# Transposed x by crossbar from HBM, weights on a second queue, z on VectorE, query normalization moved forward, LN2 sums from accumulators

## The chip, the cores and the metric

The kernel runs on one core of one Trainium2 chip. The metric is the device time of one execution in microseconds (us), as the median of several runs. The span of a profile, from the first to the last instruction, is 1.7 us shorter than the time of the same run. Engine names: PE (TensorE matmul), PEld (its weight load), DVE (VectorE), ACT (ScalarE), POOL (GpSimd), SP (the sync engine, here a DMA queue). SBUF is the on-chip memory that tiles lie in, PSUM the one that matmuls write to. A "crossbar" load or transpose is a DMA that transposes a tile on its way (DMA_TRANSPOSE in the profile). In a profile line, L608 is line 608 of the kernel, and `a<-b` says that tile a is made from b; "landing" is the moment when a DMA is complete.

## The reference, cut to what matters

```python
x = A_x                                            # [1, 2048, 640] bf16
g = sigmoid((x * gate_w).sum(-1, keepdims=True))
qkv = x @ wqkv                                     # 32 heads of 20
pq, pk = phi(q), phi(k)
kv  = einsum("bhsd,bhse->bhde", pk, v)
z   = einsum("bhsd->bhd", pk)                      # sum of pk over all 2048 tokens
o   = (pq @ kv) / ((pq * z).sum(-1) + 1e-6)
a   = o @ wo
h   = gelu(layernorm(x) @ w1)                      # LN1, W1
x1  = x + shifted(h) @ w2                          # W2
b   = x1 + gelu(layernorm(x1) @ w3) @ w4           # LN2, W3, W4
out = g * a + (1 - g) * b
```

## The kernel before

Tokens are worked on in 16 tiles of 128. The stages on PE are: Q and K (x^T times wq and wk), G (x^T pk, from which kv is made), W1, W2, W3, then per tile "A" (normalized queries times M) and W4. Each engine gets its own instruction list. The lists are made before the run by a list scheduler in the kernel's Python: it assigns a cost in ns to each instruction, simulates, and places the next item where it thinks that it can start. PE then executes that order whatever really happens (the wait of 6.39 us below shows it). The parts that matter here:

```python
def t_x(t):                     # transpose one tile of x on PE, copy PSUM -> SBUF on DVE
    b = bank()
    tr_group(b, [x_tok[:, t, 128 * k:128 * (k + 1)] for k in range(KD)])
    copy(dve, xT[:, :, 128 * t:128 * (t + 1)], psb(b, 0, D).rearrange(...))

# head loads, all on SP: rows of x, wq, rows of x, wq, wk, gate vector ...
dma_in(x_tok[:, 0:2, :], ...); load_wq(0); load_wq(1); dma_in(x_tok[:, 2:4, :], ...)
...                             # q_two: tiles 0 and 1 together, one k-slice of wq at a time
for c in range(1, NCH):         # tiles 4..15: load rows, then crossbar SBUF -> SBUF
    dma_in(x_tok[:, 4 * c:4 * c + 4, :], ...)
    for t in range(4 * c, 4 * c + 4):
        sch.dma("sp", xT[:, :, 128 * t:128 * (t + 1)], x_tok[:, t, :], ..., transpose=True)

def z_add(t):                   # 16 adds on POOL, after LN1
    tt(pool, zacc[:, :] if t < NT - 1 else zsum[:, :], zacc[:, :], pk_tok[:, t, :], ALU.add)

def zb_group():                 # PE: broadcast the sum to all partitions with a matmul of ones
    b = pair()
    mm_group(ps[:, b, 0:512], [(ones_c[:, 0:128], zsum[:, 0:512])])
    mm_group(ps[:, b + 1, 0:128], [(ones_c[:, 0:128], zsum[:, 512:D])])
    copy(dve, zb[:, :], psf[:, 512 * b:512 * b + D])
# qn_tile: five DVE instructions normalize one tile of queries with zb, then a crossbar transpose
IT.add("MISC", ("w4load",), 0.0, w4_load, deps=[(("kvt", 1), 0.0), (("t1", NT - 1), 0.0), (("z", NT - 1), 1.5)])
```

The buffer of w4 shares memory with pk_tok, so w4 can be loaded only after z is done.

## Time and profile before

| | before |
|---|---|
| time, median | 268.6 us |
| span | 267.0 us |
| PE busy | 259.9 us |
| first K tile starts | 12.56 us |
| last matmul ends | 264.19 us |

The busy table of the page:

```profile
PE 259.9 (97%) x1727; PEld 136.4 (51%) x1727; DVE 154.2 (58%) x308; ACT 95.1 (36%) x184; POOL 101.2 (38%) x153
```

PE has little idle time to give, and the other engines are far from full. The waits of PE (engine, line, what it waited for, us in total, times, longest):

```profile
PE ps L608 <- DMA pqnT<-pq_tok: 1.6, 1, 1.6
PE ps L827 <- POOL ones_c L662: 1.6, 1, 1.6
PE ps L850 <- DMA wq<-in_A_wqkv_dram: 0.7, 1, 0.7
PE ps L850 <- DVE xT L668: 0.4, 1, 0.4
```

Only the first, third and fourth could go with this change. The timeline of PE shows where the K stage starts, and the later G and W1 groups (start us, us, instructions merged):

```profile
12.56 1.75 PE L608 MATMUL ps<-wkg,xT 128*128 128x512 bf16 x11
...
70.00 1.52 PE L778 MATMUL ps<-pk_tok,x_tok 128*128 128x512 bf16 x10
71.35 1.24 PE L608 MATMUL ps<-xnT,w_61 128*128 128x512 bf16 x5
```

The z sum before (groups of instructions: busy us, mean ns of one, idle before), and the one kind of DVE reduction that this trace contains:

```profile
L636 POOL TENSOR_TENSOR zacc<-zacc,pk_tok 128x640 f32<-128x640 f32 x15 | 21.0, 1400 | 0.4
L1035 DVE TENSOR_REDUCE dnr<-qprod 128x32 f32<-128x640 f32 x16 | 13.1, 820 | 0.5
```

The second line reads 640 numbers in 820 ns.

### The profile page before, as it was taken

The numbers are of one execution on the slowest core, as the hardware profiler recorded it, in microseconds if no ns is written. First come the engines' busy times: TensorE is split into PE (matmuls) and PEld (weight loads), VectorE is DVE, ScalarE is ACT, GpSimd is POOL, SyncE is SP. The second block draws the span as 40 slices with busy tenths as digits, with TensorE's granted clock in tenths as the row PEclk, the third lists the DMA queues.
The fourth block names the chain that finished last, engine by engine and source line by source line (L and its number), as shares of the span: only waits on it lengthen the run. The fifth ranks groups of instructions, "written<-read, shape, count | busy, mean of one in ns | idle before, by whom it ended". The sixth has DMA issues, their size and how long they took to land.

```text
span 267.0 us, 4369 instructions
## 1 busy us (share of the span) xinstructions
PE 259.9 (97%) x1727; PEld 136.4 (51%) x1727; DVE 154.2 (58%) x308; ACT 95.1 (36%) x184; POOL 101.2 (38%) x153
## 2 busy tenths in 40 slices
PE   7899999999999999999999999799999999999995
PEld 3555555555454546554444555354544555545553
DVE  1597877830005667995009957879733753766533
ACT  1396677743443552614555300003322302130000
POOL 5003995756579294965950020210103010030200
PEclk9999999999999999999999999999999999999999
DMA  6755997647768211415369510411701121110411
GB/s 180 262 90 138 185 196 135 189 84 116 101 125 267 96 39 35 87 27 64 76 128 311 52 25 3 49 25 25 150 0 27 30 97 27 20 29 0 125 49 49
DMA packets 50292, 24.78 MB, mean 93 GB/s; under 512 B 41692, under 2 KB 48861, under 8 KB 50272
## 3 DMA queue, kind: packets, MB, share of 16 engines
q1 hardware_dynamic: 49120, 21.23, 36.1%
q0 software_dynamic: 1152, 3.28, 5.3%
q8 instruction: 13, 0.21, 0.4%
q14 instruction: 7, 0.06, 0.1%
HBM read 12.04 MB, written 2.62 MB: 55 GB/s over the span
## 4 chain that ended last, share of the span: by engine, by line
PE 93%; DMA 3%; DVE 2%; SPq 1%; issue 0%
PE ps L608 62%; PE ps L1096 20%; PE ps L778 8%; DMA wq<-in_A_wqkv_dram 2%; DMA pqnT<-pq_tok 1%; PE ps L1078 1%; PE ps L1026 1%; PE ps L850 1%; SPq L283 1%; PE ps L929 1%; DVE x_tok L642 1%; DVE dnr L1035 0%; DVE pq_tok L1040 0%; DVE qprod L636 0%; PE ps L619 0%
## 5 line engine op out<-in xcount | busy, mean ns | idle before, releaser
L659 ACT ACTIVATE h2T<-ps 128x512 bf16<-128x512 f32 x52 | 31.1, 597 | 84.4 <-PE ps L608 84.4
L1096 PE MATMUL ps<-w_86,h2T 128*128 128x512 bf16 (+1 forms) x416 | 58.9, 299 | 0.0
L608 PE MATMUL ps<-xnT,w_60 128*128 128x512 bf16 x260 | 58.7, 379 | 0.0
L630 POOL TENSOR_SCALAR abx<-x_tok,stg 128x640 f32<-128x640 bf16 x16 | 14.9, 935 | 109.1 <-DVE x_tok L642 60.0
L1096 PEld LDWEIGHTS ps<-w_86,h2T 128*128 128x128 bf16 x416 | 32.5, 98 | 27.6 <-issue 1.8
L608 PEld LDWEIGHTS ps<-xnT,w_60 128*128 128x128 bf16 x260 | 24.7, 98 | 27.5 <-DVE abx L642 0.3
L636 DVE TENSOR_TENSOR x_tok<-ps,x_tok 128x512 bf16<-128x512 f32 (+1 forms) x32 | 15.6, 486 | 33.7 <-PE ps L608 32.0
L642 DVE SCALAR_TENSOR_TENSOR x_tok<-ps,stg,abx 128x512 bf16<-128x512 f32 (+1 forms) x32 | 16.9, 548 | 31.2 <-PE ps L1096 31.2
L659 ACT ACTIVATE Er<-ps 128x640 bf16<-128x640 f32 x32 | 22.5, 705 | 19.2 <-PE ps L608 9.8
L659 ACT ACTIVATE hsT<-ps 128x512 bf16<-128x512 f32 (+1 forms) x32 | 18.9, 594 | 24.9 <-PE ps L608 24.5
L608 PE MATMUL ps<-M_sb,pqnT 128*128 128x512 bf16 (+1 forms) x160 | 23.9, 299 | 1.6 <-DMA pqnT<-pq_tok 1.6
L778 PE MATMUL ps<-pk_tok,x_tok 128*128 128x512 bf16 (+1 forms) x160 | 24.2, 299 | 0.0
L608 PE MATMUL ps<-wkg,xT 128*128 128x512 bf16 (+1 forms) x160 | 24.0, 299 | 0.0
L608 PE MATMUL ps<-w_62,hsT 128*128 128x512 bf16 (+1 forms) x160 | 23.9, 299 | 0.0
L608 PE MATMUL ps<-xnT,w_61 128*128 128x512 bf16 x100 | 23.9, 379 | 0.0
L642 DVE SCALAR_TENSOR_TENSOR abx<-ps,stg,abx 128x512 f32<-128x512 f32 (+1 forms) x32 | 17.5, 549 | 9.7 <-POOL abx L630 5.0
L636 POOL TENSOR_TENSOR zacc<-zacc,pk_tok 128x640 f32<-128x640 f32 x15 | 21.0, 1400 | 0.4
L608 PE MATMUL ps<-wq,xT 128*128 128x128 bf16 (+1 forms) x140 | 21.1, 299 | 0.0
L608 PEld LDWEIGHTS ps<-M_sb,pqnT 128*128 128x128 bf16 x160 | 12.9, 98 | 13.0 <-DMA pqnT<-pq_tok 1.8
L608 PEld LDWEIGHTS ps<-w_62,hsT 128*128 128x128 bf16 x160 | 13.1, 98 | 11.7
L608 PEld LDWEIGHTS ps<-wkg,xT 128*128 128x128 bf16 x160 | 12.9, 97 | 9.4
L778 PEld LDWEIGHTS ps<-pk_tok,x_tok 128*128 128x128 bf16 x160 | 12.6, 98 | 8.8
(70 smaller groups left out, 256.5 us busy)
## 6 DMA issues: line engine op xcount, KB each, us to landing
w_60<-in_B_w_dram SPq DMA_DIRECT2D x1, 2160.0 KB, 9.8
w_86<-in_B_w_dram SPq DMA_DIRECT2D x1, 2080.0 KB, 8.8
x_tok<-in_A_x_dram SPq DMA_DIRECT2D x3, 640.0 KB, 6.1
out_dram<-x_tok SPq DMA_DIRECT2D x3, 640.0 KB, 4.5
wq<-in_A_wqkv_dram SPq DMA_DIRECT2D x5, 160.0 KB, 4.7
wkg<-in_A_wqkv_dram SPq DMA_DIRECT2D x1, 800.0 KB, 7.5
wv<-in_A_wqkv_dram POOLq DMA_DIRECT2D x1, 800.0 KB, 5.4
wo_aug<-in_A_wo_dram POOLq DMA_DIRECT2D x5, 150.0 KB, 5.0
```

The lines of the kernel that those rows point to most:

```text
L283: return e.dma_start(out_ap, in_ap)
L608: ins = e.matmul(out_ap, l, r, start=(i == 0), stop=(i == n - 1))
L630: return engf(lambda e: e.tensor_scalar(out_ap, in_ap, s1, s2, op0, op1), rd, [out_ap], cost=cost)
L636: return engf(lambda e: e.tensor_tensor(out_ap, a, b_, op), [a, b_], [out_ap], cost=cost)
L642: return dve(lambda e: e.scalar_tensor_tensor(out_ap, in0, scalar, in1, op0, op1), rd, [out_ap], cost=cost)
L659: return act(lambda e: e.activation(out_ap, in_ap, func, bias=bias, scale=scale), rd, wr, cost=cost)
L778: ins = e.matmul(o, l, r, start=(t0 + q_ == 0), stop=(t0 + q_ == NT - 1))
L850: ins = e.matmul(o, l, r, start=(k == 0), stop=(k == KD - 1))
L929: ins = e.matmul(o, l, r_, start=st_, stop=sp_, skip_group_check=True)
L1026: ins = e.matmul(o, l, r, start=st, stop=sp)
L1078: ins = e.matmul(o, l, r, start=True, stop=False)
L1096: ins = e.matmul(o, l, r, start=False, stop=(i == KFF - 1))
```

## The change

Its intent: free PE from transposes in the head, take z off the POOL engine (1.40 us an add, z done at 136.6 us) so that queries can be normalized long before W4 needs them, and shorten the LN2 statistics on DVE. The diff, cut to its core (evictions in pairs of PSUM banks, the tail and bookkeeping are left out):

```diff
-    dma_in(x_tok[:, 0:2, :], x2[0:256, :]..., "x01")
-    ...  # x rows and wq, wk, gate vector, all on SP
+    def load_xT(t):
+        sch.dma("sp", xT[:, :, 128 * t:128 * (t + 1)], x2[128 * t:128 * (t + 1), :], "trx%d" % (t % 4), transpose=True)
+    for k in range(KD):
+        sch.dma("act", wq[:, k, :], A_wqkv[128 * k:128 * (k + 1), 0:D], "wq%d" % k)
+    sch.dma("act", wkg[:, :, 0:D], ...)
+    sch.dma("act", wkg[:, :, D + 2:D + 3], gate_w...)
+    for c in range(NCH):
+        for t in range(4 * c, 4 * c + 4):
+            load_xT(t)
+        dma_in(x_tok[:, 4 * c:4 * c + 4, :], ...)
-    NWARM = 5
-    NWARM2 = 2
+    NWARM = 8
-    def q_two(t0):    # tiles 0 and 1 in steps of wq
+    def q_first():    # tile 0 alone in steps of wq
@@
-    def z_add(t):
-        tt(pool, zacc[:, :] if t < NT - 1 else zsum[:, :], zacc[:, :], pk_tok[:, t, :], ALU.add)
+    def z_sum(g):
+        cs = slice(160 * g, 160 * (g + 1))
+        dve(lambda e: e.tensor_reduce(qprod[:, cs], pk_tok[:, :, cs].rearrange("p n d -> p d n"), AX.X, ALU.add),
+            ..., cost=2740.0)
+        if g == 3:
+            copy(dve, zsum[:, :], qprod[:, :])
@@ LN2
-        tt(dve, x_tok[:, t, 0:512], ...); tt(dve, x_tok[:, t, 512:D], ...); bn_stats; bn_stats; bn_aggr
+        stt(x_tok[:, t, :], psf[...], 1.0, x_tok[:, t, :], ALU.mult, ALU.add, accum=st2[:, 0, t:t + 1])
+    def w2_sq(t):
+        activation(junk[:, 0, :], x_tok[:, t, :], ACTF.Square, accum=st2[:, 1, t:t + 1])
@@ normalization of queries: now paced by W1 and W3 groups instead of W4 tiles; transposes after W2 and LN2
-        deps = [(("zb",), 1.0), (("q", max(t, 2)), 2.0), (("w2", NT - 1), 0.5)]
+        deps = [(("zb",), 1.0), (("q", t), 2.0)]
+        IT.add("QT", ("qt", t), ..., deps=[(("qn", t), 3.2), (("w2", NT - 1), 0.5), (("t2", NT - 1), 0.0)])
@@
-    w4load deps ... (("z", NT - 1), 1.5)
+    w4load deps ... (("z", 3), 1.5)
```

More of the change, by code (lines that the diff above doesn't have):

```diff
@@ L246, in simulate @@
             elif sem is not None and sem.startswith("d:"):
-                self.eng_free[eng] = t + (500.0 if eng == "sp" else 1000.0)
+                self.eng_free[eng] = t + (1000.0 if eng == "pool" else 500.0)
                 self.dma_free = max(self.dma_free, t) + nbytes / 330.0
@@ L480, in _build @@
     st2 = pa.alloc("st2", [128, 8, NT], F32)
-    bn2 = pa.alloc("bn2", [128, NT, 2], F32)
-    bns = pa.alloc("bns", [128, 4, 12], F32)
     stg = pa.alloc("stg", [128, 4, NT], F32)
@@ L499, in _build @@
     junk = pa.alloc("junk", [128, 1, D], BF16)
-    zacc = pa.alloc("zacc", [128, D], F32)
+    qprod = pa.alloc("qprod", [128, D], F32)
     zsum = pa.alloc("zsum", [128, D], BF16)
@@ L512, in _build @@
     abx = rb.alloc("abx", [128, 4, D], F32)
-    qprod = rb.alloc("qprod", [128, D], F32)
     sch.stats["sbuf"] = (pa.cur - pa.lo, pa.hi - pa.lo, ra.cur - ra.lo, rb.cur - rb.lo, ra.hi - ra.lo)
@@ L636, in tt, with stt @@
         return engf(lambda e: e.tensor_tensor(out_ap, a, b_, op), [a, b_], [out_ap], cost=cost)
-    def stt(out_ap, in0, scalar, in1, op0, op1):
+    def stt(out_ap, in0, scalar, in1, op0, op1, accum=None):
         rd = [in0, in1] + ([scalar] if not isinstance(scalar, (int, float)) else [])
@@ L641, in stt @@
         cost = (65.0 + n / 0.96) if (in_psum(in0) or in_psum(in1)) else (160.0 + 1.04 * n)
+        if accum is not None:
+            return dve(lambda e: e.scalar_tensor_tensor(out_ap, in0, scalar, in1, op0, op1, accum_out=accum), rd,
+                       [out_ap, accum], cost=cost + 70.0)
         return dve(lambda e: e.scalar_tensor_tensor(out_ap, in0, scalar, in1, op0, op1), rd, [out_ap], cost=cost)
@@ L677, in dma_in @@
         return sch.dma("sp", out_ap, in_ap, key, **kw)
-    dma_in(x_tok[:, 0:2, :], x2[0:256, :].rearrange("(n p) d -> p n d", p=128), "x01")
-    def load_wq(k):
-        dma_in(wq[:, k, :], A_wqkv[128 * k:128 * (k + 1), 0:D], "wq%d" % k)
-    load_wq(0)
-    load_wq(1)
-    dma_in(x_tok[:, 2:4, :], x2[256:512, :].rearrange("(n p) d -> p n d", p=128), "x23")
-    for k in range(2, KD):
-        load_wq(k)
-    dma_in(wkg[:, :, 0:D], A_wqkv[:, D:2 * D].rearrange("(k p) f -> p k f", p=128), "wk")
-    dma_in(wkg[:, :, D + 2:D + 3], gate_w.rearrange("(k p o) -> p k o", p=128, o=1), "gw", noncontig=True)
-    for c in range(1, NCH):
+    def load_xT(t):
+        sch.dma("sp", xT[:, :, 128 * t:128 * (t + 1)], x2[128 * t:128 * (t + 1), :], "trx%d" % (t % 4), transpose=True)
+    for k in range(KD):
+        sch.dma("act", wq[:, k, :], A_wqkv[128 * k:128 * (k + 1), 0:D], "wq%d" % k)
+    sch.dma("act", wkg[:, :, 0:D], A_wqkv[:, D:2 * D].rearrange("(k p) f -> p k f", p=128), "wk")
+    sch.dma("act", wkg[:, :, D + 2:D + 3], gate_w.rearrange("(k p o) -> p k o", p=128, o=1), "gw", noncontig=True)
+    for c in range(NCH):
+        for t in range(4 * c, 4 * c + 4):
+            load_xT(t)
         dma_in(x_tok[:, 4 * c:4 * c + 4, :], x2[512 * c:512 * (c + 1), :].rearrange("(n p) d -> p n d", p=128), "xc%d" % c)
-        for t in range(4 * c, 4 * c + 4):
-            sch.dma("sp", xT[:, :, 128 * t:128 * (t + 1)], x_tok[:, t, :], "trx%d" % (t % 4), transpose=True)
     k_done = {}
@@ L723, in _build @@
     aselect(mask[0:120], mask_t[0:120], [[20, 6], [0, 20]], ALU.is_ge, 19, -1)
-    memset(pool, zacc[:], 0.0)
     memset(pool, Lt[:], 0.0)
@@ L738, in _build @@
     IT = _Items()
-    NWARM = 5
-    NWARM2 = 2
-    def t_x(t):
-        b = bank()
-        tr_group(b, [x_tok[:, t, 128 * k:128 * (k + 1)] for k in range(KD)])
-        copy(dve, xT[:, :, 128 * t:128 * (t + 1)], psb(b, 0, D).rearrange("p (k c) -> p k c", k=KD))
+    NWARM = 8
     def phi(b, dst, after_exp=None):
@@ L786, in gt_step, with ln_chunk_stats @@
             activation(GT[:, i, :], psf[:, 512 * b:512 * b + D], ACTF.Copy)
-    def z_add(t):
-        tt(pool, zacc[:, :] if t < NT - 1 else zsum[:, :], zacc[:, :], pk_tok[:, t, :], ALU.add)
-    def ln_chunk_stats1(c):
-        cs = slice(4 * c, 4 * c + 4)
-        rs = lr[:, cs, 0:1].rearrange("p t o -> p (t o)")
-        ts(pool, st1[:, 2, cs], rs, 1.0 / D, 0.0, ALU.mult, ALU.add)
-        ts(pool, st1[:, 3, cs], st1[:, 1, cs], 1.0 / D, EPS_LN, ALU.mult, ALU.add)
-        tt(pool, st1[:, 4, cs], st1[:, 2, cs], st1[:, 2, cs], ALU.mult)
-        tt(pool, st1[:, 5, cs], st1[:, 3, cs], st1[:, 4, cs], ALU.subtract)
-        tt(pool, st1[:, 6, cs], st1[:, 5, cs], negh[:, 0:4], ALU.pow)
-        tt(pool, st1[:, 7, cs], st1[:, 2, cs], st1[:, 6, cs], ALU.mult)
-        ts(pool, st1[:, 7, cs], st1[:, 7, cs], -1.0, 0.0, ALU.mult, ALU.add)
+    def z_sum(g):
+        cs = slice(160 * g, 160 * (g + 1))
+        dve(lambda e: e.tensor_reduce(qprod[:, cs], pk_tok[:, :, cs].rearrange("p n d -> p d n"), mybir.AxisListType.X, ALU.add),
+            [pk_tok[:, t, cs] for t in range(NT)], [qprod[:, cs]], cost=2740.0)
+        if g == 3:
+            copy(dve, zsum[:, :], qprod[:, :])
+    def ln_chunk_stats(st, c, rs):
+        cs = slice(4 * c, 4 * c + 4)
+        ts(pool, st[:, 2, cs], rs, 1.0 / D, 0.0, ALU.mult, ALU.add)
+        ts(pool, st[:, 3, cs], st[:, 1, cs], 1.0 / D, EPS_LN, ALU.mult, ALU.add)
+        tt(pool, st[:, 4, cs], st[:, 2, cs], st[:, 2, cs], ALU.mult)
+        tt(pool, st[:, 5, cs], st[:, 3, cs], st[:, 4, cs], ALU.subtract)
+        tt(pool, st[:, 6, cs], st[:, 5, cs], negh[:, 0:4], ALU.pow)
+        tt(pool, st[:, 7, cs], st[:, 2, cs], st[:, 6, cs], ALU.mult)
+        ts(pool, st[:, 7, cs], st[:, 7, cs], -1.0, 0.0, ALU.mult, ALU.add)
     def gate_chunk(c):
@@ L836, in q_tile, with fn @@
         phi(b, pq_tok[:, t, :])
-    def q_two(t0):
-        bs = [pair(), pair()]
+    def q_first():
+        b = pair()
         for k in range(KD):
-            jobs = []
-            for i in range(2):
-                l = xT[:, k, 128 * (t0 + i):128 * (t0 + i + 1)]
-                jobs.append((ps[:, bs[i], 0:512], l, wq[:, k, 0:512]))
-                jobs.append((ps[:, bs[i] + 1, 0:128], l, wq[:, k, 512:D]))
-            def fn(e, jobs=jobs, k=k):
-                ins = None
-                for o, l, r in jobs:
-                    ins = e.matmul(o, l, r, start=(k == 0), stop=(k == KD - 1))
-                return ins
-            pe(fn, [wq[:, k, :], xT[:, k, 128 * t0:128 * (t0 + 2)]], [j[0] for j in jobs], cost=2 * 271.7)
-            if k == 2:
-                t_x(t0 + 2)
-                t_x(t0 + 3)
-        for i in range(2):
-            phi(bs[i], pq_tok[:, t0 + i, :])
+            l = xT[:, k, 0:128]
+            def fn(e, l=l, k=k):
+                e.matmul(ps[:, b, 0:512], l, wq[:, k, 0:512], start=(k == 0), stop=(k == KD - 1))
+                return e.matmul(ps[:, b + 1, 0:128], l, wq[:, k, 512:D], start=(k == 0), stop=(k == KD - 1))
+            pe(fn, [wq[:, k, :], l], [ps[:, b, 0:512], ps[:, b + 1, 0:128]], cost=271.7)
+        phi(b, pq_tok[:, 0, :])
     def addA(name, dur, fn, deps=()):
         IT.add("A", name, dur, fn, deps)
-    if NWARM:
-        addA(("warm",), 0.0, lambda: warmup(NWARM, 427.0))
-    for i in range(2):
-        addA(("tx", i), 0.28, lambda i=i: t_x(i))
-    if NWARM2:
-        addA(("warm2",), 0.0, lambda: warmup(NWARM2, 300.0))
-    addA(("q", 0), 2.72, lambda: q_two(0))
-    addA(("q", 2), 1.36, lambda: q_tile(2))
-    addA(("q", 3), 1.36, lambda: q_tile(3))
+    addA(("warm",), 0.0, lambda: warmup(NWARM, 427.0))
+    addA(("q", 0), 1.36, q_first)
+    for i in range(1, 4):
+        addA(("q", i), 1.36, lambda t=i: q_tile(t))
     for i in range(4):
@@ L884, in stats1 @@
     def stats1(c):
-        ln_chunk_stats1(c)
+        ln_chunk_stats(st1, c, lr[:, 4 * c:4 * c + 4, 0:1].rearrange("p t o -> p (t o)"))
         gate_chunk(c)
@@ L896, in _build @@
         IT.add("T1", ("t1", u), 0.0, lambda u=u: t_xn(1, u), deps=[(("n1", u), 1.1)])
-    for u in range(NT):
-        IT.add("Z", ("z", u), 0.0, lambda u=u: z_add(u), deps=[(("n1", NT - 1), 0.0)] if u == 0 else [(("z", u - 1), 1.5)])
+    for g in range(4):
+        IT.add("Z", ("z", g), 0.0, lambda g=g: z_sum(g), deps=[(("k", NT - 1), 2.0)])
     LAST_EXP = ("k", NT - 1)
@@ L963, in _build @@
         IT.add("KVF", ("kvt", h), 1.2 - 0.6 * h, lambda h=h: kvt_group(h), deps=[(("g", KD - 1), 1.0)])
-    for h in range(2):
         IT.add("KVF", ("lt", h), 0.0, lambda h=h: lt_evac(h), deps=[(("kvt", h), 0.0)])
@@ L967, in _build @@
         IT.add("KVF", ("m", j), 0.57, lambda j=j: m_group(j), deps=[(("lt", 0), 2.6), (("lt", 1), 1.0)] if j == 0 else [])
-    IT.add("KVF", ("zb",), 0.3, zb_group, deps=[(("z", NT - 1), 1.7)])
+    IT.add("ZB", ("zb",), 0.0, zb_group, deps=[(("z", 3), 1.7)])
     SHIFT = (1, -1, 2, -2)
@@ L979, in w1_group @@
             activation(hsT[p0:p1, j, o0:o0 + 512], ps[p0:p1, b, :], ACTF.Gelu_apprx_tanh)
-    def ln_chunk_stats2(c):
-        cs = slice(4 * c, 4 * c + 4)
-        mean = bn2[:, cs, 0:1].rearrange("p t o -> p (t o)")
-        var = bn2[:, cs, 1:2].rearrange("p t o -> p (t o)")
-        ts(pool, st2[:, 2, cs], var, 1.0, EPS_LN, ALU.mult, ALU.add)
-        tt(pool, st2[:, 6, cs], st2[:, 2, cs], negh[:, 0:4], ALU.pow)
-        tt(pool, st2[:, 7, cs], mean, st2[:, 6, cs], ALU.mult)
-        ts(pool, st2[:, 7, cs], st2[:, 7, cs], -1.0, 0.0, ALU.mult, ALU.add)
     def w2_tile(t):
         tok = slice(2 + 128 * t, 2 + 128 * (t + 1))
-        b1, b2 = bank(), bank()
-        mm_group(ps[:, b1, 0:512], [(hsT[:, k, tok], w2[:, k, 0:512]) for k in range(KD)])
-        mm_group(ps[:, b2, 0:128], [(hsT[:, k, tok], w2[:, k, 512:D]) for k in range(KD)])
-        tt(dve, x_tok[:, t, 0:512], ps[:, b1, 0:512], x_tok[:, t, 0:512], ALU.add)
-        tt(dve, x_tok[:, t, 512:D], ps[:, b2, 0:128], x_tok[:, t, 512:D], ALU.add)
-        sb_ = slot("bns", 4)
-        dve(lambda e: e.bn_stats(bns[:, sb_, 0:6], x_tok[:, t, 0:320]), [x_tok[:, t, 0:320]], [bns[:, sb_, 0:6]], cost=400.0)
-        dve(lambda e: e.bn_stats(bns[:, sb_, 6:12], x_tok[:, t, 320:D]), [x_tok[:, t, 320:D]], [bns[:, sb_, 6:12]], cost=400.0)
-        dve(lambda e: e.bn_aggr(bn2[:, t, :], bns[:, sb_, :]), [bns[:, sb_, :]], [bn2[:, t, :]], cost=110.0)
-        if t % 4 == 3:
-            ln_chunk_stats2(t // 4)
+        b = pair()
+        mm_group(ps[:, b, 0:512], [(hsT[:, k, tok], w2[:, k, 0:512]) for k in range(KD)])
+        mm_group(ps[:, b + 1, 0:128], [(hsT[:, k, tok], w2[:, k, 512:D]) for k in range(KD)])
+        stt(x_tok[:, t, :], psf[:, 512 * b:512 * b + D], 1.0, x_tok[:, t, :], ALU.mult, ALU.add, accum=st2[:, 0, t:t + 1])
+    def w2_sq(t):
+        activation(junk[:, 0, :], x_tok[:, t, :], ACTF.Square, accum=st2[:, 1, t:t + 1])
     def w3_group(c, j):
@@ L1029, in w3_half, with qn_sum @@
         activation(h2h[:, sl, :], ps[:, b, 0:256], ACTF.Gelu_apprx_tanh)
-    def qn_tile(t):
+    qn_slot = {}
+    def qn_sum(t):
         sd = slot("dnr", 4)
-        pq3 = pq_tok[:, t, :].rearrange("p (h d) -> p h d", d=DH)
         tt(dve, qprod[:, :], pq_tok[:, t, :], zb[:, :], ALU.mult)
@@ L1037, in qn_tile, with qn_scale @@
             [qprod[:, :]], [dnr[:, 0, sd, :]], cost=820.0)
+        qn_slot[t] = sd
+    def qn_scale(t):
+        sd = qn_slot[t]
+        pq3 = pq_tok[:, t, :].rearrange("p (h d) -> p h d", d=DH)
         ts(dve, dnr[:, 0, sd, :], dnr[:, 0, sd, :], EPS_PHI, None, ALU.add, ALU.bypass)
@@ L1041, in qn_tile, with qt_tile @@
             [pq3, dnr[:, 1, sd, :]], [pq3], cost=900.0)
+    def qt_tile(t):
         sch.dma("sp", pqnT[:, :, 128 * t:128 * (t + 1)], pq_tok[:, t, :], "trn%d" % slot("trn", 4), transpose=True)
@@ L1051, in a_tile @@
         tok = slice(128 * t, 128 * (t + 1))
-        b1, b2 = bank(), bank()
-        mm_group(ps[:, b1, 0:512], [(pqnT[:, j, tok], M_sb[:, j, 0:512]) for j in range(KD)])
-        mm_group(ps[:, b2, 0:128], [(pqnT[:, j, tok], M_sb[:, j, 512:D]) for j in range(KD)])
-        stt(abx[:, sa, 0:512], ps[:, b1, 0:512], stg[:, 2, t:t + 1], abx[:, sa, 0:512], ALU.mult, ALU.add)
-        stt(abx[:, sa, 512:D], ps[:, b2, 0:128], stg[:, 2, t:t + 1], abx[:, sa, 512:D], ALU.mult, ALU.add)
+        b = pair()
+        mm_group(ps[:, b, 0:512], [(pqnT[:, j, tok], M_sb[:, j, 0:512]) for j in range(KD)])
+        mm_group(ps[:, b + 1, 0:128], [(pqnT[:, j, tok], M_sb[:, j, 512:D]) for j in range(KD)])
+        stt(abx[:, sa, :], psf[:, 512 * b:512 * b + D], stg[:, 2, t:t + 1], abx[:, sa, :], ALU.mult, ALU.add)
     w4_banks = {}
@@ L1063, in w4_half @@
         pr = (t % 4) // 2
-        bs = [bank() for _ in range(4)]
-        for i in range(4):
-            bank_hold.add(bs[i])
-        w4_banks[t] = (bs[0], bs[1])
-        w4_banks[t + 1] = (bs[2], bs[3])
+        bs = []
+        for i in range(2):
+            b = pair()
+            bs += [b, b + 1]
+            w4_banks[t + i] = (b, b + 1)
+        bank_hold.update(bs)
         jobs = []
@@ L1102, in w4_tile @@
         bank_hold.discard(b2)
-        stt(x_tok[:, t, 0:512], ps[:, b1, 0:512], stg[:, 3, t:t + 1], abx[:, sa, 0:512], ALU.mult, ALU.add)
-        stt(x_tok[:, t, 512:D], ps[:, b2, 0:128], stg[:, 3, t:t + 1], abx[:, sa, 512:D], ALU.mult, ALU.add)
+        if t == NT - 1:
+            stt(x_tok[:, t, 0:512], ps[:, b1, 0:512], stg[:, 3, t:t + 1], abx[:, sa, 0:512], ALU.mult, ALU.add)
+            stt(x_tok[:, t, 512:D], ps[:, b2, 0:128], stg[:, 3, t:t + 1], abx[:, sa, 512:D], ALU.mult, ALU.add)
+        else:
+            stt(x_tok[:, t, :], psf[:, 512 * b1:512 * b1 + D], stg[:, 3, t:t + 1], abx[:, sa, :], ALU.mult, ALU.add)
     def out_tiles(t0, t1):
@@ L1132, in _build @@
         IT.add("W2", ("w2", t), 1.33, lambda t=t: w2_tile(t), deps)
+        IT.add("SQ", ("sq", t), 0.0, lambda t=t: w2_sq(t), [(("w2", t), 1.0)])
+        if t % 4 == 3:
+            IT.add("S2", ("s2", c), 0.0, lambda c=c: ln_chunk_stats(st2, c, st2[:, 0, 4 * c:4 * c + 4]), [(("sq", t), 1.0)])
     for u in range(NT):
-        deps = [(("w2", 4 * (u // 4) + 3), 5.2 + 0.9 * (u % 4))]
+        deps = [(("s2", u // 4), 3.2 + 0.9 * (u % 4))]
         if u >= 3:
@@ L1141, in _build @@
     IT.add("MISC", ("w3load",), 0.0, w3_load, deps=[(("k", NT - 1), 0.0), (("t1", NT - 1), 0.0)])
-    IT.add("MISC", ("w4load",), 0.0, w4_load, deps=[(("kvt", 1), 0.0), (("t1", NT - 1), 0.0), (("z", NT - 1), 1.5)])
+    IT.add("MISC", ("w4load",), 0.0, w4_load, deps=[(("kvt", 1), 0.0), (("t1", NT - 1), 0.0), (("z", 3), 1.5)])
     for c in range(NCH):
@@ L1146, in _build @@
             if c == 0 and j == 0:
-                deps0 = [(("kvt", 1), 0.0), (("z", NT - 1), 1.5)]
+                deps0 = [(("kvt", 1), 0.0), (("z", 3), 1.5)]
             else:
@@ L1157, in _build @@
     for t in range(NT):
-        deps = [(("zb",), 1.0), (("q", max(t, 2)), 2.0), (("w2", NT - 1), 0.5)]
-        deps.append((("w3", 0, 3 * t), 0.0) if t < 4 else (("w4", t - 4), 0.0))
-        IT.add("QN", ("qn", t), 0.0, lambda t=t: qn_tile(t), deps)
+        deps = [(("zb",), 1.0), (("q", t), 2.0)]
+        if 3 <= t < 11:
+            i = (5 * (t - 3)) // 2 + 1
+            deps.append((("w1", i // KD, i % KD), 0.0))
+        elif t >= 11:
+            deps.append((("w3", 0, 2 * (t - 11)), 0.0))
+        IT.add("QN", ("qs", t), 0.0, lambda t=t: qn_sum(t), deps)
+        IT.add("QN", ("qn", t), 0.0, lambda t=t: qn_scale(t), [(("qs", t), 0.0)])
+        IT.add("QT", ("qt", t), 0.0, lambda t=t: qt_tile(t), deps=[(("qn", t), 3.2), (("w2", NT - 1), 0.5), (("t2", NT - 1), 0.0)])
     for t in range(NT):
         c = t // 4
-        deps = [(("qn", t), 5.0), (("w4load",), 0.0), (("m", KD - 1), 1.0)]
+        deps = [(("qt", t), 3.0), (("w4load",), 0.0), (("m", KD - 1), 1.0)]
         if t >= 4:
```

## The prediction

> **What bounds it now.** TensorE. The page's busy table gives PE 259.9 of 267.0 us (97%), granted clock 1.0; the time of 268.6 us is 1.7 us above that span. By the waits and the timeline PE's idle 7.1 us are: 1.59 us at the start (ones constant), 0.36 us (DVE copy of the transposed x), 0.73 us (DMA of wq), 1.65 us at 167.6 us (DMA of the normalized, transposed queries), about 2.8 us after the last matmul. DVE (58%), ACT (36%) and POOL (38%) have slack, so moving work between them is worth only the PE waits it removes.
>
> **What the change does, with this trace's durations.**
> - Head: removes 20 PE transposes (0.98 + 0.72 us), two warm-up matmuls (0.59 us), four PSUM copies and the 1.1 us of waits around them. Adds crossbar loads: each takes the SP queue 1.2 to 1.28 us and lands 2.6 to 3.3 us after issue. wq (0.82 MB), wk and the gate vector go to the ACT queue, beside the 1.28 us table load.
> - z: 16 POOL adds (22.4 us, off the path) become 4 strided DVE reductions, estimated from 0.82 us for 640 elements at 2.7 us each, in the G stage, where DVE was busy 1.8 of 25.6 us.
> - Query normalization (0.82+0.82+0.18+0.35+0.84 = 3.0 us a tile) leaves the W4 stage for the G, W1 and W2 stages; its transposes still wait for W2's end. This removes the 1.65 us wait.
> - LN2: two adds and three batch-norm instructions (2.14 us a tile) become one accumulating DVE instruction (estimate 1.05 us) plus Square and accumulator read (0.74 + 0.20 us) on ACT.
> - Paired evictions save DVE about 0.25 us each, off the path.
>
> **On the critical path.** Only the head and the 1.65 us wait. From the first K tile (12.56 us) on there are 250.0 us of PE work that the change leaves alone; the question is when that tile can start. Four Q tiles (1.36 us each) precede it, the first in steps of wq. The removed PE work suggests 2.5 us earlier. But from 6 to 12 us the DMA engines were 93 to 99% busy. The crossbar works in 256-byte packets; 160 KB then keep the engines busy about 1.1 us, against 0.5 us in 1280-byte rows. [...] I estimate wq complete at 7 to 8.3 us, wk and gate vector at about 12 us, first K tile at 12.3 us: 0.3 us gained.
>
> New risk: DVE is nearly full from 81 to 110 us (estimate 30 us of work in 29), which may delay W2 evictions and cost PE up to 1 us; I allow 0.4.
>
> **Prediction.** 268.6 - 0.3 - 1.65 + 0.4 = 267.0 us; 8 in 10: 264.8 to 269.2. Faster by over 2% 0.03, within 2% 0.93, slower 0.04.
>
> **What would show it.** First K matmul near 12.3 us; the wait for the transposed queries gone; no PE idle between; DVE over 90% busy from 81 to 110 us; POOL under 85 us in all.
>
> **What would make it wrong.** Crossbar reads from HBM much slower than from SBUF (first K tile after 14 us); wq landing by 6 us (first K tile near 10.5, time near 265); a table load per Square on ACT; PE waiting for PSUM pairs in W2.

Where the cut is marked, a sentence is left out. 268.6 - 0.3 - 1.65 + 0.4 = 267.05, given as 267.0 us. The 0.3 us rests on an estimate which takes it that the loads of both queues share one set of busy engines; that was my assumption. The sizes behind it are in the trace before. From 13.6 to 19.6 us a 256-byte crossbar packet took 26.5 ns on average, so 640 of them on 16 engines 1.06 us; from 6.2 to 8.2 us a 1280-byte packet took 58 ns, so 128 of them 0.46 us; the DMA share from 6 to 12 us was 0.91 to 1.04, microsecond by microsecond. In that trace SCALAR_TENSOR_TENSOR took 0.82 us on 128x640, about 0.75 on 128x512 and 0.35 on 128x128, and the accumulator read of ACT 0.20 us.

## The result, and the profile after

Ratios here are the mean time of one kernel's fast runs over that of the other's of the same rounds, so they are not quite the ratio of the medians quoted. Executions over 1.5% slower than the fastest of the same kernel are left out of the means. The changed kernel takes 282.71 us (281.15 to 283.09, 4 runs) against 268.58 us: ratio 1.0515, 95% interval 1.0475 to 1.0555. It is 14 us slower, and outside the predicted range.

| | before | after |
|---|---|---|
| span | 267.0 us | 280.7 us |
| mean granted PE clock | 1.000 | 0.982 |
| first K tile starts | 12.56 us | 16.05 us |
| last block of G alone to first W2 tile | 54.26 to 81.10 us | 57.75 to 93.78 us |
| last matmul ends | 264.19 us | 277.93 us |

The table divides the loss into three: the head, 16.05 - 12.56 = 3.5 us; the G stage, (93.78 - 57.75) - (81.10 - 54.26) = 9.2 us; the rest up to the last matmul, (277.93 - 93.78) - (264.19 - 81.10) = 1.1 us. Together 13.8 us, which is the difference of the spans to 0.1 us. (The G stage now also holds the two broadcast matmuls of z, 0.3 us at full pace, which before ran at 139.69 us.) The busy table and the waits of PE:

```profile
PE 263.9 (94%) x1708; PEld 135.8 (48%) x1708; DVE 149.6 (53%) x230; ACT 106.8 (38%) x216; POOL 83.5 (30%) x148
```

```profile
PE ps L605 <- DVE zsum L668: 6.4, 1, 6.4
PE ps L836 <- DMA wq<-in_A_wqkv_dram: 2.7, 3, 1.5
PE ps L605 <- DMA pqnT<-pq_tok: 2.0, 1, 2.0
PE ps L819 <- POOL ones_c L662: 1.6, 1, 1.6
PE ps L605 <- ACT h2T L659: 0.7, 1, 0.7
PE ps L605 <- DMA xT<-in_A_x_dram: 0.5, 1, 0.5
```

PE is busy for 4 us longer although it has fewer instructions: some matmuls ran slowly. The chain of work that ended last, in order of time (start us, us, what), names the links; here only those that are not PE's own pace:

```profile
3.46 9.72 DMA xT<-in_A_x_dram
13.23 11.18 PE ps L605 x80
...
59.91 17.90 DVE qprod L779 x4
77.83 1.08 DVE zsum L668
78.96 2.85 PE ps L605 x7
...
130.82 7.49 DMA xnT<-xn
138.39 1.85 POOL xn L627
...
149.57 2.69 DMA pqnT<-pq_tok
```

A crossbar tile took 9.7 us from its issue. The four z reductions took 17.9 us, not the 11 that the prediction and the scheduler assumed. And an LN2 transpose took 7.5 us, followed at some distance by the late query transpose. The timeline of PE where the K stage starts, and around z:

```profile
16.05 5.63 PE L605 MATMUL ps<-wkg,xT 128*128 128x512 bf16 x40
...
70.25 2.32 PE L605 MATMUL ps<-xnT,w_59 128*128 128x512 bf16 x10
78.96 0.71 PE L605 MATMUL ps<-zsum,ones_c 128*128 128x512 bf16 x2 [6.39 <-DVE zsum L668]
79.46 2.34 PE L605 MATMUL ps<-xnT,w_59 128*128 128x512 bf16 x5
81.59 2.60 PE L767 MATMUL ps<-pk_tok,x_tok 128*128 128x512 bf16 x10
84.03 1.24 PE L605 MATMUL ps<-xnT,w_59 128*128 128x512 bf16 x5
```

PE stands for 6.39 us, then five W1 matmuls take 2.34 instead of 1.24 us and ten G matmuls 2.60 instead of 1.52 us. The same groups ran at the shorter durations before. The trace's records of the granted clock show half clock from 76.94 to 83.77 us, and once before, in the head, from 8.68 to 12.09 us; these 10.2 us make the mean of 0.982. In this profile the stretch in the head cost nothing by itself, since PE then still waited 0.55 us for a tile of x.

The theory from here: (1) z is late because its DVE reduction reads with a large step, and PE stands behind it because its order was fixed on a cost of 2740 ns; (2) the standstill lowers PE's clock, which adds about 2.4 us (0.2 + 1.1 + 1.1 us over the three groups from 78.96 us); (3) the head is late because crossbar and plain loads are in flight together; (4) the query transposes are late because the load of w4, which now starts earlier, runs into the LN2 transposes. Rivals are named with each run.

### The profile page after: what moved, and what is told of

It is laid out like the page before. It is cut to its first block, busy times and chain, and to the rows that moved or that the text cites. A ratio compares the mean times of both kernels' runs of the same rounds, so it can differ in the third digit from the quotient of the medians.

```text
span 280.7 us, 4283 instructions
## 1 busy us (share of the span) xinstructions
PE 263.9 (94%) x1708; PEld 135.8 (48%) x1708; DVE 149.6 (53%) x230; ACT 106.8 (38%) x216; POOL 83.5 (30%) x148
## 4 chain that ended last, share of the span: by engine, by line
PE 73%; DMA 10%; DVE 8%; POOL 5%; SPq 1%; issue 1%; ACT 1%; POOLq 0%; ACTq 0%
PE ps L605 48%; PE ps L1067 20%; DVE qprod L779 6%; DMA xnT<-xn 5%; PE ps L767 4%; DMA xT<-in_A_x_dram 3%; POOL xn L627 2%; POOL st_55 L633 2%; SPq L279 1%; PE ps L1049 1%; DMA pqnT<-pq_tok 1%; PE ps L989 1%; ACT junk L658 1%; POOL st_55 L627 1%; DVE zsum L668 0%
## 5 line engine op out<-in xcount | busy, mean ns | idle before, releaser
L605 PE MATMUL ps<-xnT,w_58 128*128 128x512 bf16 x260 | 61.2, 379 | 0.0
L642 DVE SCALAR_TENSOR_TENSOR x_tok<-ps,stg,abx 128x640 bf16<-128x640 f32 (+2 forms) x17 | 14.3, 845 | 62.6 <-PE ps L1067 62.6
L627 POOL TENSOR_SCALAR abx<-x_tok,stg 128x640 f32<-128x640 bf16 x16 | 12.7, 798 | 110.5 <-DVE x_tok L642 99.6
L642 DVE SCALAR_TENSOR_TENSOR abx<-ps,stg,abx 128x640 f32<-128x640 f32 x16 | 14.1, 884 | 34.0 <-PE ps L605 30.1
L767 PE MATMUL ps<-pk_tok,x_tok 128*128 128x512 bf16 (+1 forms) x160 | 25.3, 307 | 0.0
L605 PE MATMUL ps<-xnT,w_59 128*128 128x512 bf16 x100 | 25.1, 392 | 0.0
L605 PE MATMUL ps<-wq,xT 128*128 128x512 bf16 (+1 forms) x150 | 23.7, 306 | 0.5 <-DMA xT<-in_A_x_dram 0.5
L658 ACT ACTIVATE junk<-x_tok 128x640 bf16<-128x640 bf16 x32 | 23.6, 736 | 1.4 <-DVE x_tok L640 0.9
L627 DVE TENSOR_SCALAR Er<-Er 128x640 bf16<-128x640 bf16 x32 | 12.1, 377 | 20.6 <-ACT Er L659 20.4
L627 POOL TENSOR_SCALAR xn<-x_tok,st_55 128x640 bf16<-128x640 bf16 x16 | 17.6, 1106 | 8.7 <-DMA xnT<-xn 8.3
L605 PEld LDWEIGHTS ps<-wq,xT 128*128 128x128 bf16 x150 | 12.4, 100 | 11.9 <-issue 1.4
```

The source lines that it names most:

```text
L605: ins = e.matmul(out_ap, l, r, start=(i == 0), stop=(i == n - 1))
L627: return engf(lambda e: e.tensor_scalar(out_ap, in_ap, s1, s2, op0, op1), rd, [out_ap], cost=cost)
L642: return dve(lambda e: e.scalar_tensor_tensor(out_ap, in0, scalar, in1, op0, op1), rd, [out_ap], cost=cost)
L658: return act(lambda e: e.activation(out_ap, in_ap, func, bias=bias, scale=scale, accum_out=accum), rd, wr, cost=cost)
L767: ins = e.matmul(o, l, r, start=(t0 + q_ == 0), stop=(t0 + q_ == NT - 1))
```

## The experiments

Eleven kernels ran. All gave outputs that passed the comparison, including the two with a z that is wrong on purpose: their z sums as many values of similar size, which is presumably why the comparison did not tell.

### The wait for z: e1_zcontig, e2_zcost

```diff
-    pk_tok[:, :, cs].rearrange("p n d -> p d n")
+    pk_tok[:, 4 * g:4 * g + 4, :].rearrange("p n d -> p (n d)").rearrange("p (d n) -> p d n", n=NT)
```

> The changed kernel with one thing altered: the four DVE reductions for z read 2560 neighbouring bf16 elements instead of 16 rows at a stride of 1280 bytes (wrong result on purpose, same instruction order on every engine, same element counts). Theory S (the stride makes the reduction slow): each takes about 2.8 us instead of 4.5, z is ready near 72 us, TensorE's 6.4 us wait and the slow-clock matmuls after it go, time 282.7 - 8.9 = about 273.8 us. Rival R (the reduction costs about 1.75 ns an element whatever it reads, or POOL's normalization beside it slows it): still 4.5 us each, time unchanged near 282.7 us. Rival W (the loss is DVE being overbooked in the W1 and W2 stages): the time hardly moves even if the reductions get faster.

Measured: 274.63 us (273.69 to 275.61, 4 runs), ratio to before 1.0221. The instruction order is the same, only the addresses differ. The groups view, of the changed kernel and then of this run:

```profile
L779 DVE TENSOR_REDUCE qprod<-pk_tok 128x160 f32<-128x2560 bf16 x4 | 17.9, 4536 | 0.0
```

```profile
L779 DVE TENSOR_REDUCE qprod<-pk_tok 128x160 f32<-128x2560 bf16 x4 | 11.0, 2812 | 0.0
```

The same instruction on the same number of elements took 4.54 us with a step of 1280 bytes and 2.81 us with neighbours. The timeline of PE in e1 shows the broadcast matmul without a wait:

```profile
71.82 0.43 PE L605 MATMUL ps<-zsum,ones_c 128*128 128x512 bf16 x2
```

The wait for z is gone, and 8.1 us with it. Theory S holds; R and W fall. In the profile the G stage itself took 26.9 instead of 36.0 us, 9.1 us less; some of it was lost again later, in a wait for the query transposes of 2.9 instead of 2.0 us with half clock after it.

```diff
-            [pk_tok[:, t, cs] for t in range(NT)], [qprod[:, cs]], cost=2740.0)
+            [pk_tok[:, t, cs] for t in range(NT)], [qprod[:, cs]], cost=4560.0)
```

> The changed kernel with only the list scheduler's cost of one z reduction raised from 2740 to 4560 ns (what the trace shows), so that the broadcast matmul of z is placed later in TensorE's program. If the loss in the G stage comes from an in-order TensorE standing at a matmul whose input was promised too early, the 6.4 us wait and the slow clock after it go: about 274 us. If the late z itself is what costs (normalized queries late), it stays above 279 us and a wait for the transposed queries of several us appears at the W4 stage.

Measured: 274.19 us (272.46 to 277.40, 4 runs; the 277.40 was slow and is the one profiled; the three fast runs have a median of 274.05), ratio of the fast runs 1.0183. z is as slow as in the changed kernel (4.56 to 4.59 us a reduction), but the list now puts more G and W1 work ahead of the broadcast matmul, and PE has no wait for z. Its time is that of e1 within the noise. So the late z as such costs nothing that shows here; the fixed order behind a cost that was too low does.

### The wait or the clock: e9_fill

```diff
     def zb_group():
         b = pair()
+        pe(fill, [ones_c[:, 0:640]], [ps[:, b, :]], cost=0.0)      # 28 dummy matmuls 128x512
         mm_group(ps[:, b, 0:512], [(ones_c[:, 0:128], zsum[:, 0:512])])
```

> The changed kernel with 28 dummy matmuls (128x512, about 6 us at full clock) put on TensorE just before the broadcast matmul of z, where it stands still for 6.4 us; otherwise the same order. z comes at the same time, so the wait itself is not shortened. Theory C (the idle time lowers TensorE's clock, and the slow matmuls after it cost about 2.4 us on top of the wait): matmuls after z at full speed, about 280.3 us. Rival (the wait is all there is): 282.7 us or a little more.

Measured: 280.84 us (280.27 to 281.26, 4 runs), ratio to before 1.0438 against 1.0515 for the changed kernel. The timeline of PE:

```profile
73.76 6.21 PE L939 MATMUL ps<-ones_c 128*128 128x512 bf16 x28
80.10 0.45 PE L605 MATMUL ps<-zsum,ones_c 128*128 128x512 bf16 x2
80.38 1.24 PE L605 MATMUL ps<-xnT,w 128*128 128x512 bf16 x5
81.46 1.52 PE L767 MATMUL ps<-pk_tok,x_tok 128*128 128x512 bf16 x10
```

With useless work in the gap, the next groups run at 1.24 and 1.52 us again. The mean granted clock of this profile is 0.994, against 0.982 in the changed kernel's. About 2 us of the G stage's loss were the clock. In the trace of the changed kernel, of the 6.4 us of standstill the clock was at half for the last 2.0 us, and for 4.8 us after it, with durations up to nearly doubled (2.34 instead of 1.24 us).

### How large a step is large: e10_strides

```diff
+    src = (flat[...] step 1 element, flat[...] step 2, flat[...] step 16, pk_tok[:, :, cs] step 640)[g]
```

> The changed kernel with the four z reductions reading 2560 bf16 elements each at a different step: 2 bytes, 4 bytes, 32 bytes and 1280 bytes (wrong result on purpose). Measures the reduction alone. Theory S1 (any step beyond neighbours is slow): 2.8, 4.5, 4.5, 4.5 us. Theory S2 (only large steps are slow): 2.8, 2.8, then somewhere between, 4.5 us.

One look (277.39 us, state unknown; the time is not the point). The four reductions took 2.82, 2.81, 4.81 and 4.51 us: steps of 2 and 4 bytes took the same time, and 32 bytes cost as much as 1280. Steps of 8 and 16 bytes were not run, so where between 4 and 32 the price begins is not shown. The second forecast was the better one, but its "somewhere between" for 32 bytes was wrong. What makes the larger steps slow no run shows. The price at 1280 bytes is (4.51 - 2.81) us / 2560 = 0.66 ns an element.

### The head: e3_headold, e4_before_headnew

e3 is the changed kernel with the old head (the first block of the diff undone), e4 the kernel before with the new one.

```diff
 e3:  -  load_xT / wq, wk on ACT / q_first      +  dma_in rows of x, t_x on PE, wq on SP, q_two
 e4:  +  load_xT / wq, wk on ACT / q_first      -  dma_in rows of x, t_x on PE, wq on SP, q_two
```

> The changed kernel with the head of the kernel before: x loaded in rows, tiles 0 to 3 transposed on TensorE, wq, wk and gate vector on the SP queue. Theory: the head alone costs 3.5 us (first K tile at 16.05 instead of 12.56 us), so 282.7 - 3.5 = 279.2 us, first K tile near 12.6 us, the G stage wait still there. Rival (an early start is eaten by the wait for z): under 1 us gained. The model sees other start times, so the order of the later stages may differ by a little.

> The kernel before with the head of the change alone (x^T by crossbar from HBM, wq, wk and gate vector on the ACT queue). If the head costs the same alone: first K tile near 16 us, 268.6 + 3.5 = about 272 us. If it costs only together with the rest: within 1 us of 268.6.

Measured: e3 278.40 us (277.79 to 278.93, 4 runs), ratio 1.0361; e4 272.75 us (270.95 to 274.07, 4 runs), ratio 1.0147. First K tile at 12.35 and 15.72 us. Undone in one kernel and done alone in the other, the head is worth 4.3 and 4.1 us, so it hardly depends on the rest. (e4 and e7 also take over the changed kernel's scheduler cost of a DMA issue on ACT, 500 instead of 1000 ns.)

The start of the K stage scatters with the new head: 16.05 us in the changed kernel, 15.46 in e1, 15.72 in e4, 17.21 in e9 and 17.10 us in e10, one profile each. And the clock takes part: in e4 it was at half from 9.79 to 13.20 us, after PE had waited for wq (2.3 us in two waits), and the 30 matmuls of Q tiles 1 to 3 took 5.58 us without a wait, against 4.1 at full pace. There 1.5 of the 3.2 us are the clock, as a consequence of the late loads.

### Which part of the head: e7_queue, e8_xbar_sp

```diff
 e7 (before):  - dma_in(wq[...]); dma_in(wkg[...])      + sch.dma("act", wq[...]); sch.dma("act", wkg[...])
 e8 (changed): - sch.dma("act", wq[...]) ...            + dma_in(wq[...]) ...   # SP: tile 0, wq, tiles 1-3, wk, gate, rest
```

> The kernel before with only wq, wk and the gate vector moved from the SP to the ACT queue; x in rows and transposed on TensorE as before; same instruction order on TensorE. Theory X (the crossbar traffic makes the head slow, not the second queue): within 1 us of 268.6, first K tile within 1 us of 12.56 us. Rival Q (two queues sharing the engines delay wq and wk): first K tile 2 us or more later, 270.5 us or more.

> The changed kernel with the crossbar loads kept but all head loads on the one SP queue, in the order tile 0, wq, tiles 1 to 3, wk, gate vector, rest. Theory X (crossbar and plain loads slow each other wherever they are issued): plain 1280-byte packets still take over 100 ns while transposes are in flight, first K tile at 15 us or later, about 282 us. Rival Q (the second queue is to blame): first K tile near 12.5 us, about 279 us. The wait for z stays in both.

The windows view of 2.2 to 10.2 us, in the order before, e7, e8, changed kernel (us, busy of each engine, then PE clock, DMA share, GB/s; the share can pass 1 because packets overlap in the records):

```profile
2.20:10.20 8.00, 6.91 (x48) 3.41 (x47) 1.78 (x4) 0.15 (x1) 2.16 (x6) 1.00 0.92 282
```

```profile
2.20:10.20 8.00, 7.18 (x45) 3.71 (x44) 1.87 (x4) 1.28 (x1) 2.16 (x6) 1.00 1.00 344
```

```profile
2.20:10.20 8.00, 7.21 (x30) 2.63 (x29) 1.15 (x2) 0.98 (x2) 1.59 (x5) 1.00 0.83 188
```

```profile
2.20:10.20 8.00, 5.26 (x17) 1.60 (x16) 0.00 (x0) 1.28 (x1) 1.58 (x5) 0.90 1.12 182
```

| head | queues | first K tile | wq, issue to landing (least/median/most) | time |
|---|---|---|---|---|
| before: plain loads | one | 12.56 us | 2.9 / 4.7 / 5.5 us | 268.6 us |
| e7: plain loads | two | 13.11 us | 3.2 / 5.2 / 6.6 us | 271.03 us (270.23 to 271.44, 4 runs), ratio 1.0074 |
| e8: crossbar and plain | one | 13.83 us | 2.3 / 3.4 / 3.4 us | 281.08 us (279.35 to 282.76, 3 fast runs; a slow one took 283.73), ratio 1.0450 |
| changed: crossbar and plain | two | 16.05 us | 2.4 / 5.2 / 6.8 us | 282.71 us |

Neither part alone costs 3.5 us at the first K tile; both together do. In the changed kernel the DMA engines are the busiest of the four and move the least. From the single DMA records of the traces: from 6.2 to 8.2 us a 1280-byte packet took 58 ns on average before, 58 ns in e7, 55 ns in e8, and 175 ns in the changed kernel, where it ran beside 256-byte crossbar packets of the other queue (118 to 163 ns in e1, e4, e9 and e10, which have the same head). So theory X was right that the crossbar has a part in it and wrong in "wherever they are issued": on one queue, in e8, plain packets kept their pace of 55 ns (I had expected over 100 ns). Rival Q's mechanism fails too: two queues of plain loads moved more, 344 against 282 GB/s, and 375 against 314 GB/s from 6.2 to 10.2 us, where one queue was already busy (DMA share 0.95). On the one queue the last of these loads was issued by 6.31 us, so the later difference is hardly issue time; these are single profiles (299 to 323 GB/s in e3, e5 and e6, also on one queue), and no run tested it further. What is not separated: e8 changes the order of the loads together with the queue.

Three qualifications. In e8 the first K tile waits for wk (1.23 us in the timeline), because wk is issued only at 8.56 us, behind the crossbar loads on the same queue (3.85 us of issue for three of them); crossbar loads were cheap neither way (in the changed kernel one took 9.7 us to land). And e8 gained 2.2 us in the head, but by its fast runs only 1.6 us of time, with an interval (1.0373 to 1.0527) that overlaps that of the changed kernel: its wait for the query transposes was 3.0 instead of 2.0 us, and its clock as low as 0.976 in one fast run. e7's time of 271.03 us meets the number that I gave to rival Q, but in the profiled run not its cause: the first K tile came only 0.55 us late. The rest came much later, after a wait for the query transposes that before has as well, in the timeline of PE in e7:

```profile
170.15 1.61 PE L608 MATMUL ps<-M_sb,pqnT 128*128 128x512 bf16 x10 [2.00 <-DMA pqnT<-pq_tok]
171.56 5.34 PE L1096 MATMUL ps<-w,h2T 128*128 128x512 bf16 x26
```

That wait is 2.00 instead of 1.65 us, and the next 26 matmuls take 5.34 instead of 3.69 us: the clock fell here and did not fall before. 0.55 + 0.35 + 1.65 = 2.55 us of the 2.6 us between the spans. This accounts for the profiled run alone (clock 0.994). The other three runs of e7 had a granted clock of 1.000 and still took 270.23, 270.74 and 271.44 us, so 1.65 us of slow clock cannot be their loss; where it was, no profile shows, and for the time of e7 rival Q is not excluded. That a 2.0 us wait does not always do so is seen in the changed kernel, whose own wait of 1.97 us was followed by matmuls at full pace. The clock records show a difference. In the changed kernel's trace the times between the clock's changes are 3.41, 64.85, 6.83 and 197.97 us, whole multiples of 3.41. In e7 the whole 2.00 us lay inside one such step (168.05 to 171.46 us), 59% of it, and the clock was at half after it; in the changed kernel 1.7 us fell into one step (148.62 to 152.04 us, 50% of it) and 0.3 into the next, and the clock stayed up. In the kernel before PE stood for 30% of the step from 168.21 us (counted back from the clock's change at 267.20 us), and the clock stayed up too. The half clock of the changed kernel began after steps in which PE stood for 70% (from 5.26 us) and for all of the time (from 73.53 us). So in these traces waits of nearly the same length differed in how they fell among the steps and in what followed.

### Both repaired, and the load of w4: e5_both, e6_both_w4late

e5 is e3 and e2 together. e6 adds:

```diff
-  w4_load, deps=[(("kvt", 1), 0.0), (("t1", NT - 1), 0.0), (("z", 3), 1.5)]
+  w4_load, deps=[(("kvt", 1), 0.0), (("t1", NT - 1), 0.0), (("z", 3), 1.5), (("t2", NT - 1), 0.0)]
```

> The changed kernel with both repairs: the head of the kernel before and the corrected cost of a z reduction. If the two losses are separate they add: 282.7 - 4.2 - 8.4 = about 270.1 us, no wait for z, first K tile near 12.4 us. What is left over 268.6 us should be the wait for the transposed queries (about 2 us at the start of the W4 stage). If the losses overlap: 272 us or more.

> As e5_both, but the 2 MB load of w4 waits until the last LN2 transpose was issued, as it happened to fall in the kernel before. Theory L (in the changed kernel z frees w4's memory earlier, the load starts earlier and its traffic slows the LN2 transposes, behind which the query transposes queue): the POOL wait for LN2 transposes and TensorE's 2 us wait for the transposed queries go, about 268 us or a little less. Rival (the query transposes are late because DVE normalizes late): the 2 us wait stays, 270 us.

Measured: e5 270.21 us (270.11 to 272.35, 4 runs), ratio 1.0066; e6 268.09 us (267.92 to 268.35, 4 runs), ratio 0.9969, 95% interval 0.9952 to 0.9985. The two large losses add, as expected. The waits of PE in e6:

```profile
PE ps L829 <- POOL ones_c L662: 1.6, 1, 1.6
PE ps L605 <- ACT h2T L659: 0.7, 1, 0.7
PE ps L852 <- DMA wq<-in_A_wqkv_dram: 0.3, 1, 0.3
```

The wait for the query transposes is gone. In the changed kernel the 2 MB load of w4 was issued at 127.81 us, between the LN2 transposes, as the timeline of SP shows:

```profile
126.56 1.20 SPq L279 DMA_TRANSPOSE xnT<-xn  x1
127.81 2.17 SPq L283 DMA_DIRECT2D w_84<-in_B_w_dram  x3
130.82 1.31 SPq L279 DMA_TRANSPOSE xnT<-xn  x1
```

With this load in flight the longest of them took 7.5 us from issue to landing, and POOL, which needs its buffers back, waited up to 5.9 us. With w4 later the longest takes 4.5 us and POOL's longest wait is 2.3 us (6.2 us in e5). The load then meets the first query transposes instead (the second takes 8.4 us), and PE does not wait for these. In the kernel before, w4 was issued at 136.97 us, after the last LN2 transpose, because z ended late (at 136.6 us). In the changed kernel z is done at 78.9 us, and the load follows its next condition, the kv matmuls that end at 127.7 us. A faster z had moved a transfer into the way of the transposes that the change depends on.

### A version that beats both: e11_best

```diff
 e6 with, in the head:
-  rows of x in pairs of tiles, wq, wk, gate vector, further rows of x: all on SP
+  SP:  tiles 0, 1, 2, 3 of x, one load each (still transposed on PE)
+  ACT: wq, wk, gate vector, then the next 512 rows of x
```

> e6_both_w4late with another head without crossbar loads: the first four tiles of x alone on the SP queue as four loads; wq, wk, gate vector and the next 512 rows of x on the ACT queue; first tiles transposed on TensorE as before. e7_queue showed 370 GB/s with plain loads on both queues, but its first x rows came 0.8 us late behind the next 640 KB of x. If x comes first now: first K tile 0.5 to 1 us earlier than 12.6 us, about 267.3 us. Rival (TensorE's own head work binds): within 0.3 us of e6_both_w4late, 268.1 us. If the x loads come late again: 270 us.

Measured: 267.62 us (267.07 to 268.36, 6 runs), ratio to before 0.9955, 95% interval 0.9939 to 0.9972. First K tile at 11.99 us, against 12.67 us in e6. It is 0.3 to 0.6% faster than the kernel before, far under 2%. From e6 it is not separated: the intervals overlap, and the two K starts are one profile each, so the gain of this head over that of e6 is not shown. What stays of PE's waits is 0.7 us on ACT and the start.

## Why the prediction was wrong, point by point

- **The z reductions, and the step that failed most.** "estimated from 0.82 us for 640 elements at 2.7 us each": they took 4.54 us, because that sample read neighbours and these read with a step of 1280 bytes (e1: 2.81 us with neighbours). The larger fault is in "On the critical path. Only the head and the 1.65 us wait". I counted the reductions as work on an idle engine and did not ask which PE instruction stands behind them, nor how far the fixed order could bear an error. It bore none: 6.39 us of wait, and about 2 us of slow clock (e9). Together this is 8.1 us by e1, and e2 shows that the same slow reductions are harmless when the order knows their cost.
- **The head.** "first K tile at 12.3 us: 0.3 us gained": it was 16.05 us, and the head costs 4.3 us (e3) and 4.1 us (e4). The mechanism named, crossbar traffic in a head bound by DMA, was right; the failed term was its size. I added busy times (1.1 us a crossbar tile, 0.5 us a plain one) as if they only queued. In flight together from two queues, plain packets took 175 instead of 58 ns, wq landed 9.7 us into the run instead of 7 to 8.3, wk and the gate vector at 13.9 and 15.2 us instead of about 12, and a crossbar tile that I had landing 3 us after issue took 9.7 us. I had named a first K tile after 14 us as a way to be wrong, but with another cause, crossbar reads from HBM that are slow by themselves: in e8, on one queue, the first four landed 2.8 to 3.7 us after issue.
- **The wait for the transposed queries.** "This removes the 1.65 us wait": it became 1.97 us. The normalization did move; the load of w4 moved too and delayed the transposes (e6). I had not followed what z's end releases.
- **DVE nearly full.** I feared 1 us of waits in W2 and allowed 0.4 us. DVE was busy 22.58 of 27.00 us and 24.02 of 28.00 us in the windows from 80 and 107 us, 84 and 86% and not over 90; PE's one listed wait in W2 was 0.7 us. The size was about right by luck: PE waited there for an eviction of ACT, not of DVE.
- **Small points that held.** POOL 83.5 us (predicted under 85); no table load per Square (two loads in all); LN2's accumulating instruction with its accumulator read took 0.82 + 0.08 us, a little under the 1.05 estimated.
- **What the clock did** was not in the prediction at all. Every PE gap was counted at its own length.
- Of the 1.1 us lost after the G stage, 0.7 us is the wait on ACT and 0.3 us the balance of the two query waits; the ACT wait was not taken apart by an experiment. As the broadcast matmuls of z left this part (0.3 us), about 0.3 us more is unaccounted for.

## What to carry to other kernels

In a program whose order is fixed ahead, an instruction moved to an idle engine is on the critical path if the busiest engine has a consumer placed just where a guessed duration ends: take that duration from a trace of the same access pattern, or place the consumer later (here 2560 elements took 4.54 us with a step of 1280 bytes and 2.81 us with neighbours, and PE waited 6.39 us). Do not add up DMA busy times where crossbar and plain loads are in flight together from two queues (here a plain packet then took 175 instead of 58 ns). And when a buffer comes free earlier, look at which transfer it starts and what is in flight then (here w4 was issued at 127.81 instead of 136.97 us, and an LN2 transpose took 7.5 us).
